# Gated linear attention and a bilinear FFN on one core: tokens put in order where y leaves PSUM, and a new order of all steps

## The chip, the cores and the metric

The kernel runs on one core of one Trainium2 chip. The metric is device time in microseconds (us) of the whole kernel, inputs and output in HBM, lower is better; it is given as the median of several runs.

The engines are named as in the profile: PE (matmuls; PEld its weight loads), DVE (vector), ACT (scalar), POOL (GpSimd) and SP (the engine that only issues DMAs here).

## The reference

Two stages. The first is a recurrence over 768 positions for each of 4 batches and 8 heads, with a state of 48 x 48; the second is a bilinear FFN on the 3072 tokens that come out of it.

```python
def _attn_ref(q, k, v, alpha):               # each (4, 8, 768, 48)
    state = np.zeros((B, H, D, D))
    for t in range(S):
        state = alpha[:, :, t, :, None] * state + np.einsum('bhd,bhe->bhde', k[:, :, t], v[:, :, t])
        y[:, :, t] = np.einsum('bhd,bhde->bhe', q[:, :, t], state)

def _moe_ref(x, w_a, w_b, w_out):            # x (3072, 384), w_a, w_b (384, 1536), w_out (1536, 384)
    return (x @ w_a) * (x @ w_b) @ w_out
# x = y, transposed to (batch * position, head * 48)
```

## The kernel before

The work is cut into six chunks. A chunk covers two batches and 256 positions: batches 0 and 1 in the even chunks, 2 and 3 in the odd ones, and chunks 0 and 1, 2 and 3, 4 and 5 share their positions. A chunk gives 512 tokens to the FFN. Inside a chunk, `u` (0 or 1) is the batch and `g` (0 or 1) is the half of 128 positions. Two neighbouring positions share a partition when q, k, v and alpha are loaded (r = 0 or 1), so that a half has 64 partitions and the attention's own order of tokens in a half is (r, s), first all even positions and then all odd ones. Within a half the recurrence is done in matmul form (scores between queries and keys, masked, times v), and between halves a state is carried.

Nothing is scheduled by a compiler. A text, `PROGRAM`, lists all steps in one order with their chunk in front (`1: a 2 0 3` is step `a` of chunk 1), and a loop at the end of the kernel calls the function of each step. Every engine executes its own instructions strictly in that order, and semaphores make it wait for the others. The last digits of a PE step name the PSUM bank, of which there are eight of 512 columns; a step that takes a bank waits until its last reader has finished. Letters at the end of a step name the engine: V is DVE, S is ACT, P is POOL, Y is SP. `*` in place of a digit means both batches of the chunk (full width, 512 tokens); a digit means one (half width, 256).

The steps that the text below speaks of:

- `ld` loads q, k, v or alpha; `W` and `Wo` load the FFN's weights. Loads on POOL's queue are issued by GpSimd, on Y by SP.
- `ln`, `ra`, `l2`, `l2s`, `R`, `H`, `L` prepare the logarithms of alpha; `B`, `A2`, `AQ` are PE's cumulative sums of them (L591, L592, L633, L638); `E` are the exponentials on ACT (L667); `lv` multiplies q or k by one of them; `mq` and `mk` (L678, DVE) write the scaled queries and keys into QKp.
- `C` transposes QKp on PE (L736) and `Ce` evicts it to kqT (chunks 0 and 1); `T` does the same with a DMA transpose issued by SP (chunks 2 to 5, L767).
- `D` are the scores (L841), which read kqT; `M` masks them on DVE (L846), `Mc` copies them on ACT (L850) and `Mm` masks that copy on DVE (L854).
- `v` casts v (L785 on ACT, L787 on DVE); `K` and `K2` are the key-value products (L799, L812) and `k` updates the state on DVE; `dk`, `de`, `dr`, `dl` bring the decay of a half to where `k` reads it.
- `SB`, `SA` and `Y` add up y in two banks (L865): the parts that come from the carried state and the part inside a half. `X` (L900, L902) evicts y from PSUM into xT.
- `a` and `b` (L919) multiply a block of 128 columns of w_a or w_b with xT, `as` (L925, ACT) evicts `a`, `pr` (L933, DVE) multiplies it with `b` out of PSUM into `prod`; `o` and `oc` (L941, L952) multiply by w_out, `ot` and `otc` (L956, L958) evict, `st` and `stc` store.

Attention matmuls use a quarter of PE's array each (64 x 64), four at a time; the transposes and the FFN use the whole of it. PE's steps of different chunks stand between each other in `PROGRAM`, so that the FFN of one chunk runs while the next chunk's attention is prepared on the other engines.

Up to the change, `X` evicts both halves of a batch with one instruction and keeps the order (r, s) of the columns; `a` and `b` read 512 columns in a row; and `pr` puts the tokens in order, by writing every second element of `prod`.

Of the kernel before, what the change touches and what calls it, by code (L numbers as in the profile page):

```python
# [101 lines left out]
1: as 2 0
0: ot 2 S
1: pr 4 0
2: R 1; lv 1 q P
1: b 3 0 6; b 2 0 7; a 5 0 2; pr 3 0; b 5 0 3; as 5 0; b 1 0 5; a 1 0 1; pr 5 0; pr 2 0; a 7 0 2; as 1 0; pr 1 0
2: AQ 3
1: SB 1 6
2: lv 0 k P
1: a 10 0 5  # L110
2: lv 1 k V; ra 0; ld v * P
1: Mm 1 1 V
2: E 1 b
1: as 10 0; b 10 0 0; pr 10 0
2: mq 1 V; E 1 i
1: as 7 0; b 7 0 1
2: E 0 b; E 0 i
1: a 0 0 5
0: st 3 Y
2: dr  # L120
1: SA 1; Y 1
2: mk 1 V
1: pr 7 0; a 11 0 0; a 6 0 3; b 6 0 2; X 1 S; b 11 0 4; a 2 1 6; as 6 0; a 3 1 7; as 11 0; b 2 1 1; pr 6 0
2: lv 0 q V
1: b 4 1 0; as 2 1
2: T 1
1: pr 11 0
2: dl
0: st 0 Y
1: a 0 1 2; pr 2 1  # L130
2: mq 0 V
1: b 3 1 3; b 0 0 6; as 3 1; as 0 0; b 0 1 7; pr 3 1; a 8 0 1; a 9 0 5
0: st 1 Y
1: b 8 0 3; b 9 0 4; pr 0 0; as 0 1
2: mk 0 V
1: a 4 1 2
3: ln *
1: a 9 1 6; pr 0 1; as 8 0; b 9 1 1
3: ra 1
1: b 10 1 7; pr 8 0; a 10 1 3; as 4 1; as 9 0; as 9 1; a 6 1 6; b 6 1 2; b 11 1 5; pr 4 1; as 10 1; pr 9 0; a 11 1 4; pr 10 1; pr 9 1; as 6 1  # L140
2: v 1 S
1: a 8 1 3; b 8 1 1; a 7 1 6; pr 6 1
3: l2 0 V
1: as 11 1
2: T 0
1: as 8 1; a 5 1 4
3: ra 0
1: as 5 1; a 1 1 2
2: v 0 V
4: ld a * Y  # L150
1: pr 11 1; as 7 1; pr 8 1
2: K2 * * 0 7; D 1 1 3; D 1 0 5
1: as 1 1; b 5 1 2; o 2 0 1
2: k * 0 V
1: pr 5 1
3: v 0 S; v 1 S
1: b 1 1 2
2: Mc 1 0; M 1 1
3: l2s 0 P; l2s 1 P
1: b 7 1 0; o 2 1 -; pr 1 1; o 3 0 4  # L160
2: SB 0 5
1: pr 7 1
3: R 0
2: D 0 0 2
1: ot 2 V
2: Mm 1 0 V
1: o 3 1 -
2: Mc 0 0; SB 1 0; D 0 1 2
3: R 1
1: ot 3 S  # L170
2: SA 0
1: o 0 0 4
0: cs 0 0 P
2: Mc 0 1
4: ln *
3: ld q * Y; ld k * Y
2: k * 1 V
3: AQ 2
2: Y 1; SA 1; Mm 0 1 V; Mm 0 0 V; Y 0; X 0 S
3: E 0 b  # L180
4: l2 0 V
2: X 1 V
1: o 0 1 -
2: b 1 * 6; a 1 * 5
3: E 1 b
# [48 lines left out]
3: D 1 0 1; D 1 1 3
2: as 10 *
3: k * 1 V; Mc 1 1
2: o 0 0 7; o 2 0 0
3: M 1 0
5: ln *
2: pr 10 *  # L240
4: lv 1 q P
3: SB 1 3; D 0 1 1; Mc 0 1
4: lv 1 k P
5: ld q * Y
1: st 0 Y
3: SB 0 5
2: o 2 1 -
3: Mm 1 1 V; Mm 0 0 V; Mm 0 1 V
4: ld v * P
2: ot 2 S; o 0 1 -  # L250
4: AQ 0; E 0 b; E 0 i
3: SA 0; Y 0; SA 1
4: E 1 b
3: Y 1
5: l2s 1 V
4: mq 0 V; mk 0 V
3: X 0 S; X 1 S
2: o 3 0 2; o 3 1 -
4: T 0
3: a 5 * 3  # L260
4: E 1 i; v 0 S
3: a 9 * 0
2: ot 3 S
3: b 5 * 6; a 6 * 5; as 5 *
2: st 2 Y
3: as 9 *
5: ld k * P; l2s 0 P
3: as 6 *
5: ra 1
# [12 lines left out]
3: b 1 * 7; as 1 *; a 3 * 5; b 9 * 6; pr 9 *; b 6 * 4; a 2 * 0; pr 6 *
4: T 1
5: lv 0 k P
3: b 0 * 6; as 0 *; as 2 *
4: dl
3: a 8 * 1
5: lv 1 q P
3: b 4 * 0; a 4 * 4; b 2 * 3; pr 1 *; pr 0 *; as 8 *; pr 2 *; as 4 *; pr 4 *; b 3 * 6; b 8 * 2
5: ld v * P; lv 1 k P  # L290
3: a 11 * 1
5: ra 0
3: as 3 *; pr 8 *; as 11 *; a 7 * 0
4: D 1 0 3; K * 0 5
5: lv 0 q P
3: pr 3 *; as 7 *
5: v 1 V
4: k * 0 V
5: R 1
4: D 1 1 6; D 0 1 1; Mc 1 0; Mc 1 1; M 0 1  # L300
2: o 1 0 0; o 1 1 -
3: a 10 * 7; b 11 * 3
4: SB 1 4
2: ot 1 S
3: as 10 *
# [72 lines left out]
5: b 11 * 1
# [26 lines left out]
def kernel(  # L405
# [11 lines left out]
    nc = tc.nc  # L417
# [681 lines left out]
```

## Time and profile before

| | |
|---|---|
| Three runs | 193.74, 194.33, 194.84 us; median 194.33 us |
| Profiled execution, first to last instruction (span) | 192.0 us, which is 2.3 us under the median; the profile gives no other time for this execution |
| PE, DVE, ACT, POOL busy | 186.8, 133.1, 106.5, 56.9 us |
| Granted TensorE clock | 1.00 over the span, full from 6.0 us after the start on |
| HBM read, written | 25.98 MB, 4.74 MB |
| DMA transposes | 8, issue to landing 4.3 to 5.9 us |
| Last matmul ends | 188.65 us |

The profile is of one execution. Its page has the busy time of each engine, the span in 40 slices, the DMA queues, the chain of waits that ended last, the costliest groups of instructions (line, engine, operation, written tile, read tiles, shapes, count; then busy time and the mean ns of one; then the idle time of the engine ahead of them and what ended it) and the DMA issues with their time to landing. The trace behind it answers further: the pieces of the chain in order of time (start, length, what), a timeline (start, length, engine, line, operation, and in brackets the idle time of the engine before it), groups by form, and the instructions of one line or tile.

### The profile page before, as it was taken

Reading aid. Unit: us, or ns where it says so; the run is one execution under the profiler, and the core shown is the slowest. Engines: PE = TensorE matmul, PEld = TensorE weight load, DVE = VectorE, ACT = ScalarE, POOL = GpSimd, SP = SyncE. Lnnn points to the kernel's source line nnn. Section 1 sums busy time; section 2 is a strip of 40 time slices with the busy share of each in tenths; the row PEclk is TensorE's granted clock in tenths of the full one; section 3 lists DMA queues with packets and bytes.
Section 4 is the critical chain, followed back from the end, with each engine's and each line's share of the span. In section 5 each row is a group of like instructions: output and inputs, shape, how many; then the busy total and the mean of one; then the engine's idle time right before and its main releaser. Section 6 shows DMA issues by size and latency. Waiting matters only on the chain.

```text
span 192.0 us, 6086 instructions
## 1 busy us (share of the span) xinstructions
PE 186.8 (97%) x2613; PEld 116.9 (61%) x2613; DVE 133.1 (69%) x223; ACT 106.5 (55%) x194; POOL 56.9 (30%) x75
## 2 busy tenths in 40 slices
PE   7999999999999999999999999999999999999992
PEld 3888875677778876645557444656465644545562
DVE  2387698994989888899897956887567446252510
ACT  4448885656779867753487756743572435314211
POOL 8999626752450500640074262000000000000000
PEclk9999999999999999999999999999999999999999
DMA  5999999999969999999999989017641200000422
GB/s 132 274 219 218 251 253 235 244 269 264 251 107 166 165 216 265 248 254 149 233 213 181 156 174 129 3 42 140 146 66 44 85 0 0 0 0 3 164 82 82
DMA packets 62618, 29.40 MB, mean 153 GB/s; under 512 B 53712, under 2 KB 60768, under 8 KB 62592
## 3 DMA queue, kind: packets, MB, share of 16 engines
q0 software_dynamic: 18432, 13.37, 39.6%
q1 hardware_dynamic: 44016, 15.55, 38.1%
q8 instruction: 20, 0.33, 0.7%
q10 hardware_dynamic: 144, 0.10, 0.2%
q14 instruction: 6, 0.05, 0.1%
HBM read 25.98 MB, written 4.74 MB: 160 GB/s over the span
## 4 chain that ended last, share of the span: by engine, by line
PE 91%; DMA 5%; SPq 1%; DVE 1%; issue 1%; ACT 0%; DVEq 0%
PE psum L919 47%; PE psum L941 24%; PE psum L865 7%; PE psum L841 3%; DMA kqT<-QKp 3%; DMA q_t<-in_q_dram 3%; PE psum L736 2%; PE psum L633 1%; PE psum L952 1%; SPq L549 1%; PE psum L799 1%; PE psum L812 1%; PE psum L700 1%; PE psum L591 1%; PE psum L592 1%
## 5 line engine op out<-in xcount | busy, mean ns | idle before, releaser
L919 PE MATMUL psum<-xT,wb_t 128*128 128x512 bf16 (+1 forms) x270 | 56.0, 337 | 0.0
L919 PE MATMUL psum<-xT,wa_t 128*128 128x512 bf16 (+1 forms) x270 | 56.0, 337 | 0.0
L941 PE MATMUL psum<-wo_t,prod 128*128 128x384 bf16 x276 | 49.4, 326 | 0.0
L919 PEld LDWEIGHTS <-wb_t 128*128 128x128 bf16 x270 | 25.9, 98 | 19.9 <-issue 0.5
L919 PEld LDWEIGHTS <-wa_t 128*128 128x128 bf16 x270 | 25.9, 98 | 19.7 <-issue 0.3
L941 PEld LDWEIGHTS <-prod 128*128 128x128 bf16 x276 | 25.9, 98 | 17.6
L956 ACT ACTIVATE ot<-psum 128x384 f32<-128x384 f32 (+1 forms) x16 | 7.7, 482 | 22.7 <-PE psum L941 21.6
L850 ACT ACTIVATE m<-psum 128x1024 bf16<-128x1024 f32 x14 | 14.1, 1023 | 4.6 <-PE psum L841 4.3
L613 POOL TENSOR_TENSOR l<-la 64x384 f32<-64x384 f32 x7 | 7.8, 1108 | 26.6 <-ACT la L556 19.0
L846 DVE TENSOR_TENSOR m<-psum,mask 128x1024 bf16<-128x1024 f32 x10 | 12.1, 1220 | 3.1 <-PE psum L841 3.1
L652 POOL TENSOR_TENSOR q_t<-q_t,ra 128x384 f32<-128x384 f32 x5 | 6.1, 1215 | 22.5 <-ACT ra L645 19.7
L556 ACT ACTIVATE la<-a_t 128x1536 f32<-128x1536 f32 (+2 forms) x9 | 9.5, 1055 | 2.3 <-DMA a_t<-in_alpha_dram 2.2
L678 DVE TENSOR_TENSOR QKp<-q_t,beta 128x768 bf16<-128x768 f32 x10 | 10.0, 995 | 1.0 <-ACT beta L667 1.0
L865 PE MATMUL psum<-m,vx 64*64 64x128 bf16 x576 | 10.5, 217 | 0.0
L900 ACT ACTIVATE xT<-psum 128x768 bf16<-128x768 f32 x9 | 7.2, 816 | 5.7 <-PE psum L865 5.5
L678 DVE TENSOR_TENSOR QKp<-k_t,invb 128x768 bf16<-128x768 f32 x10 | 9.7, 972 | 0.8 <-ACT invb L667 0.8
L854 DVE TENSOR_TENSOR m<-m,mask 128x1024 bf16<-128x1024 bf16 x14 | 9.3, 684 | 1.2 <-ACT m L850 1.2
L958 DVE COPY ot<-psum 128x384 f32<-128x384 f32 (+1 forms) x9 | 4.8, 532 | 7.6 <-PE psum L941 4.7
L865 PEld LDWEIGHTS <-vx 64*64 64x64 bf16 x576 | 9.0, 107 | 0.5 <-issue 0.3
L841 PE MATMUL psum<-kqT 64*64 64x128 bf16 x384 | 9.0, 219 | 0.4 <-DMA kqT<-QKp 0.3
L652 POOL TENSOR_TENSOR k_t<-k_t,a_t 128x384 f32<-128x384 f32 x6 | 7.4, 1228 | 6.1 <-issue 3.3
L549 POOL DMA_DIRECT2D v_t<-in_v_dram x8 | 8.5, 1058 | 0.1
(271 smaller groups left out, 287.9 us busy)
## 6 DMA issues: line engine op xcount, KB each, us to landing
out_dram<-ot SPq DMA_DIRECT2D x23, 192.0 KB, 3.8
q_t<-in_q_dram SPq DMA_DIRECT2D x3, 768.0 KB, 6.5
a_t<-in_alpha_dram POOLq DMA_DIRECT2D x2, 768.0 KB, 15.2
k_t<-in_k_dram POOLq DMA_DIRECT2D x2, 768.0 KB, 12.1
v_t<-in_v_dram POOLq DMA_DIRECT2D x4, 384.0 KB, 7.0
a_t<-in_alpha_dram SPq DMA_DIRECT2D x2, 768.0 KB
k_t<-in_k_dram SPq DMA_DIRECT2D x2, 768.0 KB
a_t<-in_alpha_dram POOLq DMA_DIRECT2D x3, 384.0 KB, 8.5
```

The costliest lines, as they stand in the source:

```text
L549: eng.dma_start(out=t[:, us, hs].rearrange("p b h r d -> p (b h) (r d)"), in_=src[ch.b0 + us.start:ch.b0 + us.stop, hs, ch.s * 2 * C:(ch.s ...
L556: nc.scalar.activation(out=ch.la[:, us, hs].rearrange("p b h r d -> p (b h r d)"), in_=ch.a[:, us, hs].rearrange("p b h r d -> p (b h r d) ...
L613: eng.tensor_add(ch.l2[(1 - g) * HC:(2 - g) * HC, 1], x[:, :, 0, :], x[:, :, 1, :])
L652: eng.tensor_mul(x, x, by)
L678: eng.tensor_mul(QKp[ch.c % 2][:, u, j, :, hs, :D], src[:, u, hs].rearrange("p h r d -> p r h d"), f)
L841: nc.tensor.matmul(s2[g * HC:(g + 1) * HC, r, p, rk, :], lhsT=turned_part(ch, u, 1, rk, 2 * h + p, g, rs), rhs=queriesT(ch, u, 2 * h + p, ...
L846: nc.vector.tensor_mul(m.rearrange("p r a k s -> p (r a) (k s)"), ch.s2[u, h].rearrange("p r a k s -> p (r a) (k s)"), maskn(4))
L850: nc.scalar.activation(out=m.rearrange("p r a k s -> p (r a) (k s)"), in_=ch.s2[u, h].rearrange("p r a k s -> p (r a) (k s)"), func=AF.Copy)
L854: eng.tensor_mul(x, x, maskn(4))
L865: nc.tensor.matmul(y[c * DP:(c + 1) * DP, g, j // 2 * C:(j // 2 + 1) * C], lhsT=lhsT, rhs=rhs, start=(g, c) not in begun, stop=False, skip ...
L919: nc.tensor.matmul(p, lhsT=(wa_t, wb_t)[w][:, kk, f * 128:(f + 1) * 128], rhs=ch.xT[:, kk, us, :], start=(kk == 0), stop=(kk == KT - 1))
L941: nc.tensor.matmul(op, lhsT=ch.prod[:, f, at:at + C], rhs=wo_t[:, f, :], start=(f == 0), stop=(f == NFF - 1))
```

## The change

The eviction `X` now takes one half `g` at a time, `X u g engine`, 384 columns each, and writes them in order of tokens: the reading side goes through PSUM in a row and the writing side takes every second element. xT is laid out by half (128 partitions x 4 halves x 3 blocks of 128 rows x 128 tokens), so the moving operand of a full `a` or `b` comes in four pieces of 128 columns, of a half-width one in two. `pr` then has three plain operands, and the two functions that made views for it are gone.

```diff
-    def evac(ch, u, eng):
+    def evac(ch, u, g, eng):
         if not hasattr(ch, "xT"):
-            ch.xT = wk.tile([128, KT, B, C], BF16, name="xT")
-        o_ = ch.xT[:, :, 2 * u:2 * u + 2, :].rearrange("p a g s -> p g a s")
-        i_ = ch.y[u][0][:, :, :KT * C].rearrange("p g (a s) -> p g a s", a=KT)
-        if eng is nc.scalar:
-            nc.scalar.activation(out=o_, in_=i_, func=AF.Copy)
-        else:
-            eng.tensor_copy(o_, i_)
+            ch.xT = wk.tile([128, B, KT, C], BF16, name="xT")
+        evict(ch.xT[:, 2 * u + g].rearrange("p a (s r) -> p a r s", r=2),
+              ch.y[u][0][:, g, :KT * C].rearrange("p (a r s) -> p a r s", a=KT, r=2), eng)
...
-    def tokens(x, us):
-        return x.rearrange("p (b s r) -> p b r s", s=HC, r=2)[:, us]
-
-    def columns(x, n):
-        return x.rearrange("p (b r s) -> p b r s", r=2, s=HC)
...
-            nc.tensor.matmul(p, lhsT=(wa_t, wb_t)[w][:, kk, f * 128:(f + 1) * 128], rhs=ch.xT[:, kk, us, :], start=(kk == 0), stop=(kk == KT - 1))
+            nc.tensor.matmul(p, lhsT=(wa_t, wb_t)[w][:, kk, f * 128:(f + 1) * 128], rhs=ch.xT[:, us, kk, :], start=(kk == 0), stop=(kk == KT - 1))
...
-        o_, a_, b_ = tokens(ch.prod[:, f, :], us), columns(a[:, :n], n), columns(b, n)
-        nc.vector.tensor_mul(o_, a_, b_)
+        nc.vector.tensor_mul(ch.prod[:, f, us.start * C:us.stop * C], a[:, :n], b)
```

`PROGRAM` is new as a whole. It has the same steps with three differences: 24 evictions `X` (17 on ACT, 7 on DVE) in place of 12 (9 and 3); the casts of v are 6 on ACT and 6 on DVE, by batch, instead of 9 and 3; and some evictions changed engine (`ot` 17 on ACT and 6 on DVE instead of 15 and 8, `otc` both on ACT instead of one each, `Ce` 3 on ACT and 5 on DVE instead of 2 and 6). The order, the PSUM banks and the place of the transposes among the other steps are different throughout. The beginning, and the parts with the DMA transposes of chunks 2 and 4:

```diff
-0: ... fill 7 2; cu2 V; cz 0 q V; cus; ld k 0b Y; ld k 0a Y; B 0b 5; ld q 0b Y; ld v 0 P
-0: ln 0a; ld q 0a Y; E 0b b; E 0b i; mq 0b V; B 0a 0; E 0a i; dk 0 2; E 0a b; ld a 1 P; mk 0b V; C 0 1 5; ... v 0 S; mk 0a V; cm 1
-0: de 0; fill 2 1; mq 0a V; C 0 0 3; Ce 0 1 V; ... Ce 0 0 V; D 0 1 4; ln 1; ... K 0 0 6; k 0 0 V; M 0 1; D 0 0 0; SB 0 6
-0: cz 1 q P; B 1a 2; ...
+0: ... c1; fill 7 0; cz 0 q V; ln 0a; ci; ld k 0b Y; ld k 0a Y; cu; cu2 V; cus; cz 1 b P; B 0b 2
+0: E 0b i; mk 0b V; E 0b b; ld q 0b Y; B 0a 0; ld v 0 P; mq 0b V; dk 0 2; ld q 0a Y; C 0 1 3; fill 2 4; E 0a b; mq 0a V; E 0a i; mk 0a V; ld a 1 P; C 0 0 0; v 0 S
+0: K 0 0 1; cs 0 m P; Ce 0 1 V; D 0 1 4; Ce 0 0 V; D 0 0 6; ld k 1 P; de 0; ld q 1 P; k 0 0 V; cm 1; M 0 0; SB 0 0; M 0 1; W b 0 256; ln 1; B 1a 2; E 1a b
...
-2: mk 1 V
-1: pr 7 0; a 11 0 0; a 6 0 3; b 6 0 2; X 1 S; ...
-2: T 1
...
-2: mk 0 V
...
-2: T 0
...
-2: K2 * * 0 7; D 1 1 3; D 1 0 5
...
-2: D 0 0 2
+2: mk 1 V
+1: a 6 0 3; a 11 0 0; ...
+2: mk 0 V
...
+2: mq 0 V
...
+2: dr; v 0 V; T 1; K2 * * 4 5
+1: pr 8 0; as 6 1
+2: D 1 0 1; Mc 1 0
...
+2: T 0
...
+2: D 1 1 6; M 1 1; D 0 0 2; Mc 0 0
...
-4: mq 0 V; mk 0 V
-3: X 0 S; X 1 S
-2: o 3 0 2; o 3 1 -
-4: T 0
-3: a 5 * 3
...
-4: D 0 0 3
+4: mk 0 V; T 0
+3: a 9 * 3; as 9 *
...
+4: D 0 1 4; M 0 1
```

GpSimd's queue holds the same list of instructions in the same order as before.

More of the change, by code (lines that the diff above doesn't have):

```diff
@@ new lines @@
+0: as 3 0; pr 3 0
+1: ld v 0 P; l2 1 V
+0: b 3 1 0; pr 3 1
+1: ld q 1 P
+0: Wo 0 6
+1: ld k 1 P
+0: a 5 1 2; as 0 1; pr 0 1; a 10 * 3; as 10 *; Wo 6 12; b 10 * 0; b 11 * 5
+1: H 1 V; L 1 V
+0: pr 10 *
+1: E 0 i; dk * 3
+0: as 11 *; pr 11 *
+2: ld a * P
+0: as 5 1
+1: lv 0 q V
+0: pr 5 1; b 1 1 0; a 2 1 2
+1: A2 1 5
+0: a 1 1 7
+1: de *; ld v 1 P
+0: a 6 * 3
+1: E 1 i; E 1 b
+0: b 6 * 6; as 1 1
+1: lv 0 k V; mk 0 V
+0: pr 1 1; a 7 * 5
+1: E 0 b
+0: b 2 1 0
+1: v 0 S
+0: as 2 1; a 9 * 4; as 6 *; as 9 *
@@ new lines @@
+2: ld q * P
+1: mq 0 V; C 0 1 7
+0: pr 2 1; pr 6 *
+1: Ce 0 1 S
+0: b 9 * 0; pr 9 *; b 7 * 4; as 8 *
+1: K2 0 0 2 3; k 0 0 V
+2: ld k * P
+0: as 7 *; pr 7 *
+1: D 0 1 6; M 0 1
+0: o 0 0 0
+1: C 0 0 1
+0: b 8 * 2; pr 8 *; o 1 0 4
+1: ra 1; lv 1 q V
+3: ld v * P
+1: Ce 0 0 S; SB 0 6
+0: cz 1 v P
+1: lv 1 k P; mk 1 V
+0: c3 P
+1: D 0 0 1; Mc 0 0
+0: o 0 1 -; o 2 0 5
+3: ld a * P
+1: mq 1 V; C 1 1 1
+0: ot 0 S
+1: C 1 0 0
+0: o 2 1 -
+1: Mm 0 0 V
+2: ln *; ra 1
+0: cs 1 0 P
+1: Ce 1 0 S; k 0 1 V; Ce 1 1 V
@@ new lines @@
+0: o 1 1 -; ot 1 S
+2: l2s 0 P
+0: ot 2 S
+1: SA 0; Y 0; X 0 1 S; X 0 0 S
+2: l2 0 V
+1: v 1 V
+2: l2s 1 P
+1: D 1 1 0; Mc 1 1; K2 1 1 2 3
+0: o 3 0 4; o 3 1 -
+1: a 10 0 5; as 10 0; a 3 0 0
+2: ra 0
+1: D 1 0 6; as 3 0
+0: ot 3 S
+2: R 0; R 1
+1: k 1 0 V; k 1 1 V
+2: AQ 1; E 0 i
+1: b 3 0 3; a 1 0 0; as 1 0; M 1 0
+0: st 3 Y
+1: pr 3 0; b 1 0 4; pr 1 0; b 10 0 5; pr 10 0; SB 1 6; Mm 1 1 V
+2: lv 1 q P; E 1 b; mq 1 V; lv 1 k V; lv 0 k P
+1: a 5 0 0; as 5 0; b 5 0 3; pr 5 0
+2: E 0 b
+1: a 4 0 4; b 7 0 5; as 4 0
@@ new lines @@
+2: SB 1 4
+1: pr 11 1
+2: D 0 1 6
+3: l2 0 V; R 0; R 1; ld q * Y
+2: Mc 0 1; Mm 0 1 V
+4: ln *
+1: o 3 0 1; o 3 1 -; ot 3 V
+2: Mm 0 0 V
+3: AQ 6
+4: l2 0 V
+3: E 1 b
+2: SA 1; Y 1; X 1 0 S
+4: l2s 0 P
+3: v 1 V
+2: SA 0
+3: ld k * Y; lv 0 k P
+4: ld k * Y
+2: Y 0; X 0 0 V
+1: o 0 0 1; o 0 1 -
+3: E 0 b
+1: st 3 Y
+3: dr
+2: X 0 1 S; X 1 1 S; a 1 * 2; as 1 *; b 1 * 3
+4: ld q * Y
+3: E 0 i
+2: a 3 * 4; b 2 * 2
+1: ot 2 S
+2: a 4 * 0
+3: lv 1 k V; lv 0 q P; mq 0 V
+2: a 2 * 5; as 2 *
+3: E 1 i
+2: b 3 * 6
@@ new lines @@
+3: lv 1 q V; dl
+2: pr 1 *
+3: mk 0 V
+2: b 11 * 3; pr 2 *; b 4 * 5; a 11 * 2
+4: l2s 1 P
+2: a 9 * 7
+0: st 2 Y
+2: as 4 *; as 11 *; b 9 * 0
+3: mk 1 V; T 0; mq 1 V; T 1
+2: pr 4 *
+5: ld a * Y
+2: pr 11 *
+4: R 0
+2: b 6 * 2
+1: ot 0 V
+2: a 8 * 5; as 9 *; pr 9 *
+4: ra 1
+2: a 7 * 3; a 6 * 7; as 3 *; pr 3 *; as 6 *; pr 6 *
+1: o 1 0 4
+2: as 8 *
+4: lv 1 q P
+3: K2 * * 0 1
+5: ld q * Y
+3: k * 0 V; D 0 0 6; Mc 0 0; k * 1 V
+2: a 0 * 2
+1: st 2 Y
+2: as 7 *; as 0 *; b 8 * 5; pr 8 *
+1: o 1 1 -; ot 1 V
@@ new lines @@
+2: b 7 * 0; pr 7 *; a 10 * 1
+3: Mm 0 0 V; SB 1 2; D 1 1 4; D 1 0 6; M 1 0
+2: as 10 *; b 0 * 0; pr 0 *
+3: Mc 1 1
+2: a 5 * 1; as 5 *; b 5 * 4
+4: lv 0 k V
+3: SB 0 6; SA 1
+2: pr 5 *
+4: lv 1 k P
+3: D 0 1 0
+2: b 10 * 5
+3: Mc 0 1
+2: o 2 0 4
+3: Mm 1 1 V; Y 1
+4: R 1; AQ 0; E 0 b; ld v * P
+3: Mm 0 1 V
+4: v 0 S
+3: Y 0
+2: pr 10 *
+3: X 1 1 S; X 1 0 V; SA 0; X 0 1 V; X 0 0 S
+4: E 1 i; mk 1 V; E 0 i
+1: st 0 Y
+4: E 1 b; ra 0; lv 0 q V; mq 0 V
+2: o 2 1 -; o 0 0 5
+5: ln *
+3: a 3 * 2
+4: mk 0 V; T 0
@@ new lines @@
+3: a 9 * 3; as 9 *
+4: v 1 V
+3: b 4 * 0
+4: mq 1 V
+2: ot 2 V
+5: l2s 1 V; l2 0 V
+3: a 11 * 1
+2: o 3 0 6
+3: a 4 * 3
+2: o 0 1 -
+5: ld k * P
+3: as 11 *
+4: dr
+3: a 6 * 1; b 9 * 4; pr 9 *; as 6 *; b 11 * 7; pr 11 *
+2: ot 0 S
+3: a 7 * 1; b 3 * 4
+5: l2s 0 P
+3: as 3 *; pr 3 *; b 6 * 2; pr 6 *
+5: R 0; R 1
+3: b 1 * 7; a 1 * 4; as 1 *; as 4 *; a 8 * 2; a 0 * 5
+5: ra 1
+2: st 2 Y
+4: T 1
+3: pr 4 *
+5: lv 0 k P
+3: b 0 * 4; b 5 * 3; pr 1 *; as 0 *; pr 0 *; a 5 * 0; b 8 * 7; as 5 *; pr 5 *
@@ new lines @@
+3: as 10 *; pr 10 *
+2: st 3 Y
+5: E 1 i; mk 1 V
+4: a 3 * 1
+3: pr 7 *; o 3 1 -
+4: a 6 * 3; b 0 * 6
+5: v 0 V
+4: as 7 *; as 6 *
+2: st 0 Y
+3: o 2 0 4
+4: a 0 * 3; as 0 *
+5: mq 1 V; T 0
+4: pr 7 *; pr 0 *; pr 6 *; as 3 *; a 1 * 2; as 1 *; b 3 * 7; pr 3 *; a 4 * 3; as 4 *
+3: o 2 1 -; ot 2 S
+4: b 1 * 1; pr 1 *
+5: T 1; D 1 1 2; D 1 0 4
+3: ot 3 S
+5: D 0 0 6; M 1 0; Mc 0 0; K * 0 0; dl; k * 0 V; Mm 0 0 V
+3: o 1 0 1; o 1 1 -; ot 1 V
+5: SB 0 4; SB 1 6; Mc 1 1; D 0 1 2; M 0 1; Mm 1 1 V
+3: st 2 Y
@@ new lines @@
+3: st 1 Y
+4: as 2 *; b 2 * 7; b 5 * 0; pr 2 *; pr 5 *
+5: b 3 * 2; a 3 * 7
+4: o 3 0 0
+5: as 3 *; pr 3 *
+4: o 0 0 1
+5: b 0 * 2; as 0 *; pr 0 *; as 1 *; b 1 * 3; b 9 * 6
+4: o 1 0 2; o 1 1 -
+5: a 6 * 7
+4: o 0 1 -
+5: pr 1 *; b 6 * 3; as 5 *; b 5 * 4
+4: ot 1 S
+5: b 7 * 2
+4: o 3 1 -; ot 0 S; st 0 Y
+5: as 6 *
+4: ot 3 V; st 3 Y; o 2 0 7; o 2 1 -
+5: pr 5 *; o 0 0 4; as 7 *; a 9 * 5; a 10 * 0; pr 7 *; pr 6 *; b 10 * 1; as 10 *; pr 10 *
+4: ot 2 S
+5: as 9 *
+4: st 1 Y
+5: o 3 0 2; oc 1 1 0 3; o 2 0 5
@@ L401 @@
+4: st 2 Y
+5: pr 9 *; o 0 1 -; ot 0 S; st 0 Y; o 3 1 -; ot 3 S; oc 1 1 1 -; otc 1 1 S; o 2 1 -; ot 2 S; st 3 Y; st 2 Y; stc 1 1 S; oc 1 0 0 0; oc 1 0 1 -; otc 1 0 S; stc 1 0 Y
 """
```

427 lines of the change are left out of this document (86 added, 341 removed).

## The prediction

> **What bounds the kernel now.** I read the page's busy time and slices first, then the groups by form, then the chain of waits in order of time, then the timeline of the first 20 us.
>
> ```profile
> span 192.0 us, 6086 instructions
> PE 186.8 (97%) x2613; PEld 116.9 (61%) x2613; DVE 133.1 (69%) x223; ACT 106.5 (55%) x194; POOL 56.9 (30%) x75
> PE   7999999999999999999999999999999999999992
> ```
>
> PE is busy in every slice but the first and the last; no other engine passes 69%. A busy PE is not yet a PE at its rate, so I price its work from the chain of waits, whose pieces run from one matmul's end to the next:
>
> ```profile
> 19.34 3.41 PE psum L919 x30
> 28.04 0.35 PE psum L638 x2
> 72.50 0.29 PE psum L865 x12
> 100.74 0.17 PE psum L865 x12
> 106.47 4.99 DMA kqT<-QKp
> 135.85 5.18 PE psum L919 x24
> ```
>
> 24 full-width matmuls take 5.18 us, 0.216 each, so a full `a` or `b` step (three) costs 0.65 us and a half-width one 0.33. Twelve quarter-array matmuls cost 0.17 us behind others of their kind and 0.29 behind whole-array work, so each change of kind costs about 0.11. With such prices (output half 0.98, scores step 0.23, `Y` 0.68) I add up PE's steps in the order of the program: 182.05 us. The clock of the trace minus this sum is then the time PE has lost so far. It is 5.53 us at 28.04 (`A2` of chunk 1), 5.59 at 102.96 (`AQ` of chunk 4), 5.86 at 111.50, and 6.60 at the last output matmuls. So PE loses 5.5 us at the start, nothing for 75 us, 0.3 at one wait, and 0.7 in crumbs behind it. That wait is a DMA transpose:
>
> ```profile
> 111.50 0.42 PE L841 MATMUL psum<-kqT 64*64 64x128 bf16 x16 [0.29 <-DMA kqT<-QKp]
> ```
>
> **PE's own work.** The two built programs hold the same 2,549 matmuls in the same shapes, with the same 49 changes between whole- and quarter-array work; the sum in the new order is again 182.05 us. Nothing is gained or lost there, unless the moving operand of `a` and `b`, which now comes in pieces of 128 columns, streams slower. The trace has such a pair: scores (L841) read two pieces of 64 columns and `Y` (L865, m) one of 128; their means are 219 and 217 ns. Over 540 matmuls 2 ns would be 1.1 us, the upper end; both have a median of 216, and I take 0. A gain is excluded: the same columns pass.
>
> **The eviction of y.**
>
> ```profile
> L900 ACT ACTIVATE xT<-psum 128x768 bf16<-128x768 f32 x9 | 7.2, 816 | 5.7 <-PE psum L865 5.5
> L902 DVE CAST xT<-psum 128x768 bf16<-128x768 f32 x3 | 2.9, 952 | 2.4 <-PE psum L865 2.4
> L956 ACT ACTIVATE ot<-psum 128x384 f32<-128x384 f32 x15 | 7.4, 492 | 21.7 <-PE psum L941 21.6
> L958 DVE COPY ot<-psum 128x384 f32<-128x384 f32 x8 | 4.4, 554 | 4.7 <-PE psum L941 4.7
> ```
>
> Nine ACT instructions of 0.816 and three on DVE of 0.952 become 17 of about 0.492 and 7 of about 0.554 (the output evictions have the new size): +1.0 us of busy time on each engine. Off the path, if the lead covers it: I count PE's work between the last matmul into y and the first `a` or `b` that reads xT. Before, the shortest lead is 0.70 us (chunk 0, `X 1`), under the 0.82 that the eviction takes, so up to 0.15 is lost there. After, the shortest is 1.10, with ACT and DVE taking one half each (0.55), and elsewhere 1.7 to 3.4: nothing is lost. No row of ACT shows writes in steps of two elements. From below 0.492; from above twice the time per element, 0.84 ns x 384 = 0.32 more (slope between 816 and 492); I take the lower end, nearest to DVE's interleaved products below. Even 0.81 fits into 1.10. The price is then 5.4 us of ACT time, which has 45% free; 0.5 us on the path is my upper end.
>
> **The products.** `pr` writes in a row instead of interleaved.
>
> ```profile
> L829 DVE TENSOR_TENSOR tmp<-psum,S 128x384 f32<-128x384 f32 x4 | 2.2, 552 | 1.2 <-PE psum L812 0.7 <-PE psum L799 0.6
> L829 DVE TENSOR_TENSOR tmp<-psum,Sm 128x192 f32<-128x192 f32 x4 | 1.4, 353 | 0.1
> L933 DVE TENSOR_TENSOR prod<-as__704,psum 128x512 bf16<-128x512 bf16 x1 | 0.7, 733 | 0.0
> ```
>
> Plain DVE work with one operand in PSUM has 1.04 ns per element and 0.154 fixed (552 and 353), so 0.683 for 512 against 0.733 now. 54 x 0.045 + 36 x 0.02 = 3.2 us of DVE time fewer. Three casts of v leave ACT (0.85 each) for DVE (0.35). DVE is 9.6 of 10 us busy between 80 and 90 us, so this can remove crumbs, 0 to 0.5 us; I take 0.2. The Trainium skill (SBUF — State Buffer, Door 1: The DMA port swizzle) says that accesses run at full rate while they hit the same 16-byte line again, so that bf16 may be strided by up to 8 elements for free. By it the interleaved writes cost nothing, the products stay at 0.73 and the 0.2 is nil. The rows differ by 7%, though of other shapes, and I go by the rows.
>
> **The start.** `mk 0b` now comes ahead of `mq 0b`:
>
> ```profile
> 7.81 0.56 DVE L678 TENSOR_TENSOR QKp<-q_t,prod 128x384 bf16<-128x384 f32 x1 [3.63 <-DMA q_t<-in_q_dram]
> 8.94 0.62 PE L736 MATMUL psum<-ident,QKp 128*128 128x128 bf16 x8 [0.15 <-DVE QKp L678]
> 10.80 0.84 ACT L556 ACTIVATE la<-a_t 128x768 f32<-128x768 f32 x1 [0.43 <-DMA a_t<-in_alpha_dram]
> 12.03 0.59 PE L591 MATMUL psum<-la,ut 128*128 128x192 f32 x2
> 12.86 0.77 POOL L529 DMA_DIRECT2D wb_t<-in_moe_w_b_dram  x1
> wb_t<-in_moe_w_b_dram POOLq DMA_DIRECT2D x1, 384.0 KB, 7.6
> ```
>
> k has landed while DVE waits for q, so the four products end about 0.3 earlier; `K 0 0` in front of the scores waits for v's cast (10.12), which gives some back. `B 1a` can start at 11.65 (10.80 + 0.84) instead of 12.03: 0.35 gained. But `b 5 0` needs w_b's columns 256 to 768, which land at 12.86 + 7.6 = 20.45; GpSimd's queue has the same order. In the new order 15.14 us of PE work stand before it, so PE has lost at least 5.3 there, restart included 5.35: 0.2 of the 0.35 remain.
>
> **The transposes.** `T 0` of chunk 4 had 6.05 us of PE work between its last product `mk 0` and the first scores that read it; now 13.7. The 0.3 of the one wait goes. What is late next: chunk 2's two transposes, whose lead falls from 10.6 and 10.0 us to 7.55 and 6.9. Less the product itself (0.95), 6.6 and 5.95 remain; before, issue to landing took 4.4 and 5.9 there (all eight: 4.3 to 5.9). It just fits: 0. Chunk 5's shortest lead rises from 2.3 to 3.7, where DVE has run ahead of the order. The queues of SP and GpSimd keep nearly their order (a store fewer ahead of chunk 2's second transpose; three stores ahead of chunk 5's two instead of two between them, 0.4 us each to issue, hidden by that lead).
>
> **The end.** The last store moves from ACT's queue to SP's, which must be woken: +0.05.
>
> **Sum.** -0.2 (start) -0.3 (transpose) -0.2 (crumbs) +0.05 = -0.65 on a span of 192.0. The span lies 2.3 us under the median of 194.33; with the same 2.3 the forecast is **193.7**.
>
> **Rivals.** *A. More:* all crumbs go, since DVE is lighter and evictions start by halves; PE then ends 5.4 us behind its sum instead of 6.6: -1.2, 193.1. For it: 75 us without a loss in the trace. Against: the crumbs lie where chunk 4 and 5 hand over, and the new order has them too.
>
> *B. The products don't get shorter* and DVE takes up 1.0 us for evictions and 1.05 for v: crumbs come back as large as the gains, 194.3, no change. For it: the cited rule. Against: 733 over 683.
>
> *C. Slower:* chunk 2's transposes come late. PE's next scores stand behind them in order, and each us past 5.95 from issue to landing costs PE one. For it: 5.9 was seen at that very place, and four large loads follow in SP's queue. At 8 us: +2.0 - 0.65, 195.7. Against: 4.4 for the first of the two.
>
> **Numbers.** Forecast (193.7, own range 193.3 to 194.2) 0.45; A 0.22; B 0.18; C and other losses, such as slower streaming or ACT writes, 0.15. The range 192.9 to 195.2 takes in A, B and the cheap half of C. About 0.5%, 1 us, can be told from no change: faster takes A and the low edge of the forecast, 0.30; slower takes most of C and a tail of B, 0.17; within 0.53.
>
> **What would show it.** In the new profile: PE without a wait on kqT past 100 us; products near 0.69; xT evictions of 0.49 and 0.55; B 1a at 11.65; the last matmul at about 188.0. Wrong it is if PE waits on kqT near 64 or 69 us, if full-width matmuls take more than 0.216, or if DVE's products stay at 0.73.

## The result and the profile after

The changed kernel takes 196.19 us (median of four runs, 195.96 to 197.11), the kernel before 194.06 (also four runs). The ratio is 1.0117, with a 95% interval of 1.0079 to 1.0155: the change costs 2.1 us. The forecast was 193.7 with a range of 192.9 to 195.2, so the result lies outside, on the slow side. The profiled execution took 195.96 us with a span of 194.2, and the last matmul ends at 191.15 instead of 188.65.

The page of the changed kernel, first the busy time:

```profile
span 194.2 us, 6085 instructions
PE 187.6 (97%) x2612; PEld 116.7 (60%) x2613; DVE 136.3 (70%) x226; ACT 105.6 (54%) x203; POOL 57.2 (29%) x75
```

DVE should have become lighter, since its 90 products are shorter now. It is 3.2 us busier. The groups by form show that the products did what was forecast, and that ACT's evictions are longer:

```profile
L906 ACT ACTIVATE xT<-psum 128x384 bf16<-128x384 f32 x17 | 9.2, 599 | 5.2 <-PE psum L826 5.1
L883 DVE TENSOR_TENSOR prod<-as__1915,psum 128x512 bf16<-128x512 bf16 x1 | 0.7, 681 | 0.0
```

So something else on DVE has grown. What PE waits for is listed in the waits of PE (line, what ended the wait, us in total, times, longest; the first row, a wait at the very start that the kernel before has too, and the last one are left out):

```profile
...
PE psum L870 <- DVE ot L908: 0.7, 1, 0.7
PE psum L826 <- issue: 0.5, 1, 0.5
PE psum L870 <- ACT as__486 L876: 0.4, 1, 0.4
PE psum L870 <- DMA wa_t<-in_moe_w_a_dram: 0.3, 1, 0.3
PE psum L870 <- DVE prod L883: 0.2, 1, 0.2
...
```

The wait for a DMA transpose at 111.5 us, the only large one of before, is not in this list; a wait of 0.7 for DVE has come in its place. The timeline around it, DVE, GpSimd and PE in turn (start, length, instruction):

```profile
109.63 1.16 DVE L748 COPY vx<-v_t 128x768 bf16<-128x768 bf16 x1
110.71 1.75 DVE L639 TENSOR_TENSOR QKp<-q_t,beta 128x768 bf16<-128x768 f32 x1
112.39 0.54 DVE L908 COPY ot<-psum 128x384 f32<-128x384 f32 x1
...
108.97 1.60 POOL L574 TENSOR_TENSOR l<-la 64x384 f32<-64x384 f32 x1 [14.78 <-ACT la L517]
110.66 0.99 POOL L613 TENSOR_TENSOR k_t<-k_t,a_t 128x384 f32<-128x384 f32 x1
...
112.98 1.46 PE L870 MATMUL psum<-xT,wb_t 128*128 128x512 bf16 x6 [0.69 <-DVE ot L908]
```

The same two instructions at other places of the same trace, with no GpSimd instruction beside them:

```profile
77.99 0.34 DVE L748 COPY vx<-v_t 128x768 bf16<-128x768 bf16 x1
...
87.33 0.94 DVE L639 TENSOR_TENSOR QKp<-q_t,beta 128x768 bf16<-128x768 f32 x1
```

The cast of v takes 1.16 us instead of 0.34, and the queries' product 1.75 instead of 0.94. Both start while a product of GpSimd runs, and they end 0.22 and 0.81 after that product's end (110.57 and 111.65), about what they take by themselves: they have stood until then. DVE loses 1.6 us here, its next eviction is that much late, and PE, which needs the evicted bank, stands for 0.69.

To find all such places I compared each DVE instruction with the shortest one of the same line, tiles and shape in the same trace and added up what it had more, where that was over 0.12 us. In the kernel before this gives 2.4 us, in the changed kernel 7.2. Without it DVE would be busy 130.7 us before and 129.1 after, lighter as forecast. Nine instructions of the changed kernel stand for 0.65 to 0.82 each; all overlap a product on GpSimd. Four of the nine lie between 45 and 53 us, where PE does not wait at all, so there it cost nothing. DVE instructions with an operand in PSUM, some forty of which overlap GpSimd's products in the two traces, have at most 0.03 more.

What that is to PE is seen in two stretches, 70 to 90 and 90 to 115 us (columns: length, then busy us and instructions of PE, PEld, DVE, ACT, POOL). First the kernel before, then the changed one:

```profile
70.00:90.00 20.00, 20.00 (x277) 11.17 (x276) 18.32 (x27) 11.77 (x20) 5.23 (x4) 1.00 1.12 241
90.00:115.00 25.00, 24.71 (x401) 13.50 (x400) 20.85 (x29) 15.99 (x27) 10.39 (x9) 1.00 1.02 189
```

```profile
70.00:90.00 20.00, 19.52 (x288) 11.06 (x287) 16.78 (x25) 12.71 (x23) 5.84 (x5) 1.00 1.11 217
90.00:115.00 25.00, 24.13 (x384) 13.32 (x383) 22.91 (x34) 13.75 (x23) 6.79 (x6) 1.00 0.97 189
```

Before, PE lost 0.29 in these 45 us, after, 1.35. The last matmul ends 2.50 us later than before. These 45 us give 1.07 of that, of which 0.46 is the wait named "issue", which no semaphore explains. Another 0.6 is idle time in the first 30 us, which differs from one execution to the next (see below), and 0.8 is PE's busy time itself, 187.6 instead of 186.8 us; what makes it longer was not found.

### The profile page after: what moved, and what is told of

It reads as the page before. It is cut to its first block, busy times and chain, and to the rows that moved or that the text cites. A ratio compares the mean times of both kernels' runs of the same rounds, so it can differ in the third digit from the quotient of the medians.

```text
span 194.2 us, 6085 instructions
## 1 busy us (share of the span) xinstructions
PE 187.6 (97%) x2612; PEld 116.7 (60%) x2613; DVE 136.3 (70%) x226; ACT 105.6 (54%) x203; POOL 57.2 (29%) x75
## 5 line engine op out<-in xcount | busy, mean ns | idle before, releaser
L870 PE MATMUL psum<-xT,wb_t 128*128 128x512 bf16 (+1 forms) x270 | 56.8, 337 | 1.1 <-DVE ot L908 0.7
L891 PE MATMUL psum<-wo_t,prod 128*128 128x384 bf16 x276 | 49.9, 326 | 0.0
L574 POOL TENSOR_TENSOR l<-la 64x384 f32<-64x384 f32 x7 | 9.2, 1307 | 38.9 <-ACT la L517 34.2
L906 ACT ACTIVATE ot<-psum 128x384 f32<-128x384 f32 (+1 forms) x19 | 8.8, 473 | 14.6 <-PE psum L891 14.0
L906 ACT ACTIVATE xT<-psum 128x384 bf16<-128x384 f32 x17 | 9.2, 599 | 5.2 <-PE psum L826 5.1
L639 DVE TENSOR_TENSOR QKp<-q_t,beta 128x768 bf16<-128x768 f32 x10 | 10.5, 1045 | 1.9 <-ACT invb L628 1.8
L815 DVE TENSOR_TENSOR m<-m,mask 128x1024 bf16<-128x1024 bf16 x14 | 10.2, 737 | 1.2 <-ACT m L811 1.2
L613 POOL TENSOR_TENSOR q_t<-q_t,ra 128x384 f32<-128x384 f32 x5 | 5.4, 1077 | 17.0 <-ACT ra L606 16.4
L908 DVE COPY ot<-psum 128x384 f32<-128x384 f32 x6 | 3.3, 549 | 6.4 <-PE psum L891 6.4
```

The lines of the kernel that those rows point to most:

```text
L574: eng.tensor_add(ch.l2[(1 - g) * HC:(2 - g) * HC, 1], x[:, :, 0, :], x[:, :, 1, :])
L613: eng.tensor_mul(x, x, by)
L639: eng.tensor_mul(QKp[ch.c % 2][:, u, j, :, hs, :D], src[:, u, hs].rearrange("p h r d -> p r h d"), f)
L815: eng.tensor_mul(x, x, maskn(4))
L870: nc.tensor.matmul(p, lhsT=(wa_t, wb_t)[w][:, kk, f * 128:(f + 1) * 128], rhs=ch.xT[:, us, kk, :], start=(kk == 0), stop=(kk == KT - 1))
L891: nc.tensor.matmul(op, lhsT=ch.prod[:, f, at:at + C], rhs=wo_t[:, f, :], start=(f == 0), stop=(f == NFF - 1))
```

## The experiments

The theory to be tested, called P below: DVE instructions that read and write only SBUF stand still while GpSimd works on a product; the new order puts more of them there. Its rivals: the new eviction costs (E), DVE is simply loaded too much (L), the weights land later (W). The results in one table; "standing" is the sum described above, "PE busy" is of the 45 us from 70 to 115, both in the one execution that was profiled. Each ratio is to runs of the kernel before that were taken with it; their median is 194.06 down to "six products to DVE" and 193.96 below it.

| Kernel | Median, us | Ratio to before (95%) | Standing, us | PE busy, us |
|---|---|---|---|---|
| before | 194.06 | | 2.4 | 44.71 |
| changed | 196.19 | 1.0117 (1.0079 to 1.0155) | 7.2 | 43.65 |
| eviction alone | 194.06 | 0.9998 (0.9980 to 1.0016) | 2.3 | 44.56 |
| order alone | 196.02 | 1.0093 (1.0072 to 1.0115) | 6.5 | 43.52 |
| first FFN steps swapped | 196.63 | 1.0120 (1.0096 to 1.0144) | 5.7 | 43.36 |
| six products to DVE | 197.52 | 1.0187 (1.0148 to 1.0226) | 3.4 | 41.95 |
| the same, loads held back | 195.86 | 1.0088 (1.0067 to 1.0109) | 3.2 | 44.40 |
| half an output step moved | 196.17 | 1.0120 (1.0094 to 1.0146) | 5.9 | 43.15 |
| GpSimd cleared | 194.75 | 1.0039 (1.0020 to 1.0058) | 2.1 | 44.45 |
| cleared, half step moved | 194.56 | 1.0032 (1.0018 to 1.0046) | 2.7 | 45.00 |
| before, one product to DVE | 194.13 | 1.0008 (0.9991 to 1.0024) | 3.0 | 44.93 |
| before, dummy products | 195.13 | 1.0059 (1.0038 to 1.0081) | 4.6 | 43.84 |
| before, dummy memsets | 193.89 | 0.9998 (0.9986 to 1.0009) | 2.4 | 44.66 |

Neither column alone puts the kernels in the order of their times: where DVE stands and what PE meets at the start count too.

**Which half of the change.** The first kernel is the one before, in its own order, with only the eviction by halves, the new xT and the plain products (the functions as in the change):

```diff
-0: ... X 0 S; ...
+0: ... X 0 0 S; X 0 1 S; ...
```

> The kernel before, in its own order, with the new eviction alone: X by halves in the order of tokens (each X u e becomes X u 0 e; X u 1 e), xT by halves, plain products. Theory P with W (the order costs, by collisions of DVE with GpSimd and by weights that land later): 193.7 to 194.5, no change, products 0.68, xT evictions on ACT 0.60, on DVE 0.59. Rival E: the eviction costs, 195 or more, with PE gaps in front of the first a or b of each chunk.

It is level with the kernel before. ACT's evictions take 0.607 (18 of them) and PE waits once for one, 0.2. The eviction costs nothing and gains nothing; E falls.

The second has the changed kernel's order with the old eviction, one `X u e` where the later half stood, the old xT and the interleaving products:

```diff
-2: SA 1; Y 1; X 1 0 S
+2: SA 1; Y 1; X 1 S
```

> The changed kernel's order with the eviction of before: one X for a batch at the place where its later half stood, xT in its old layout, interleaving products. Theory P with W: the order alone brings the loss, 195.7 to 197 (products 0.05 us longer each, DVE busier by 3), PE gaps near 77, 93 and 113 us again. Rival E: 194.3, as before the change.

By the medians it brings 1.96 of the 2.1 us. Cast and queries' product are long again:

```profile
109.59 1.16 DVE L748 COPY vx<-v_t 128x768 bf16<-128x768 bf16 x1
110.67 1.75 DVE L639 TENSOR_TENSOR QKp<-q_t,beta 128x768 bf16<-128x768 f32 x1
```

The new `PROGRAM` alone makes the loss. Its order and its choice of engines, such as the casts that went from ACT to DVE, are not told apart by this.

**The start.** The waits for `wa` and the one named as ACT's `as` at 21.1 us looked like weights that land late:

```diff
-0: ... SB 1 6; a 1 0 0
-0: as 1 0; a 5 0 2; as 5 0; a 4 0 1; b 1 0 3; pr 1 0; as 4 0; b 5 0 4; b 0 0 5; a 3 0 0; ... a 0 0 1; pr 5 0
+0: ... SB 1 6; a 5 0 0
+0: as 5 0; a 1 0 2; as 1 0; a 4 0 1; b 1 0 3; pr 1 0; as 4 0; b 0 0 5; a 3 0 0; ... a 0 0 1; b 5 0 4; pr 5 0
```

> The changed kernel with another order of the first FFN steps of chunk 0: a 5 ahead of a 1 (w_a's columns 256 to 768 land first), b 0, a 3 and a 0 ahead of b 5 (w_b's columns 256 to 768 land last). Theory W: PE's gaps at 19.5 (0.41 beyond a change of kind) and 21.4 us (0.48) are waits for these landings, which other steps now cover: -0.8, 195.4. Rival: the second gap is a wait for ACT's eviction of a 4, as the profile names it; then it stays and the gain is 0.3 or less, 195.9.

Both waits are gone from its trace, and it is no faster; W falls as a cause. The waits at the start differ from one execution to the next: with one and the same start the wait for `wb` was 0 in the kernel with half an output step moved and 1.3 in the one with the loads held back. In the first 30 us PE is busy 27.0 to 28.4 us in five profiled executions with the start of before, and 26.7 to 28.4 in seven with the new one; the means are 27.76 and 27.67.

**GpSimd's products away.** Six products that stood beside the long DVE instructions go to DVE:

```diff
-4: l2s 0 P        +4: l2s 0 V
-4: l2s 1 P        +4: l2s 1 V
-4: lv 1 q P       +4: lv 1 q V
-4: lv 1 k P       +4: lv 1 k V
-5: l2s 0 P        +5: l2s 0 V
-5: lv 0 k P       +5: lv 0 k V
```

> Against the changed kernel (196.2 us) only six small GpSimd products (l2s of chunk 4 twice and of chunk 5 once, lv 1 q and lv 1 k of chunk 4, lv 0 k of chunk 5) go to DVE. Theory P (port): DVE instructions with all operands in SBUF stand still while GpSimd works; the four that did so between 76 and 112 us (0.75, 0.81, 0.70, then 0.82 and 0.81 us too long) cost PE 0.53 + 0.12 + 0.23 + 0.74 = 1.6 us. Then these PE gaps (77.5, 85.5 and 87.0, 93.7, 113.4) are gone, DVE takes six times 0.55 more and some 3.9 less, and the time is about 194.6. Rival E (the new eviction is what costs): 196.2, the gaps elsewhere. Rival L (DVE is simply loaded too much): 3.3 us more on DVE makes it slower, over 196.7.

Slower, and not for any reason on the list. The cast takes 0.35 again and the queries' product 0.95, as P has it, but PE waits elsewhere, as the timelines of DVE and of PE show:

```profile
113.40 0.35 DVE L748 COPY vx<-v_t 128x768 bf16<-128x768 bf16 x1
113.67 0.95 DVE L639 TENSOR_TENSOR QKp<-q_t,beta 128x768 bf16<-128x768 f32 x1
...
95.06 0.42 PE L802 MATMUL psum<-kqT 64*64 64x128 bf16 x16 [2.48 <-DMA kqT<-QKp]
```

GpSimd, with less to do, starts the loads of v and k at 82.10 and 88.04 instead of 91.83 and 93.02, and chunk 3's first transpose, issued at 85.4, lands only at 95.0. In the changed kernel it was issued at 86.0 and landed 5.6 us later. So GpSimd's products had also held its loads back. Behind this wait the trace has something that no other profile here shows: the granted clock of PE is 0.50 from 95.92 to 99.33 us. This execution is the slowest of its six (199.54 us, median 197.52), and the other five list a mean clock of 0.999 or 1.0 instead of 0.991, so the median holds less than this trace shows.

The next kernel holds them back by a copy of one element that reads the finished transpose:

```diff
+3: gatet 0
 4: R 1; AQ 0; E 0 b; ld v * P
```

> The same six GpSimd products on DVE as in the run before, and one tiny GpSimd copy that reads kqT of chunk 3's batch 0 ahead of the load of v of chunk 4, so that the two loads on GpSimd's queue start as late as in the changed kernel (91.8 and 93.0 us) and not at 82.1 and 88.0, where they ran into chunk 3's transposes (landing 95.1, PE idle for 2.5 us). Theory P: the wait at 95 goes and the gaps at 85, 87, 94 and 113 us (0.12, 0.23, 0.74) stay away: 1.1 under the changed kernel, 195.1; the gap at 77.4 stays (next run). Rival L: DVE's 3.3 us more bring new gaps of the same size: 196.2.

The waits at 85 to 113 stay away, and a new collision takes half of the gain, with a product that had been left on GpSimd (118.94 to 119.93); the timeline of DVE and of PE:

```profile
119.10 1.24 DVE L614 TENSOR_TENSOR k_t<-k_t,a_t 128x384 f32<-128x384 f32 x1
...
120.99 0.81 PE L871 MATMUL psum<-xT,wb_t 128*128 128x512 bf16 x3 [0.49 <-DVE prod L884]
```

The gain is 0.3 instead of the expected 1.1, so this kernel alone settles nothing about P. It differs from the one before it by nothing but the later loads, and the wait at 95 is gone: the loads had delayed the transpose.

**The gap without a releaser.** PE stands 0.5 at 77 us in the middle of `Y 1` of chunk 2 with no semaphore to explain it ("issue"). Two kernels ask about it:

```diff
-0: ... fill 2 4; ...
+0: ... warm 8 4; ...
```

> The changed kernel with 8 dummy matmuls of 128 columns in the place of 2 of 512, at 9.6 us, about as long, so that every later PE instruction stands 12 places further down (6 weight loads, 6 matmuls). Theory F (fetch): the gap of 0.53 at 77.3 us comes in the middle of chunk 2's Y 1, behind its 33rd matmul and without a releaser, in four kernels of this order at PE's 2497th instruction, give or take one: it is the edge of a block of 256 instructions that PE fetches by DMA and that is not there yet. Then it comes six matmuls earlier, behind the 27th. Rival M: the 34th matmul waits for its operand (a mask by DVE): the gap stays behind the 33rd. Time as the changed kernel, 196.2.

Neither came: the gap is gone from `Y 1` altogether. The operands are the same, so a wait of the 34th matmul for its mask would have stayed. What comes instead is a wait of `Y 0` for a mask that stands beside a product of GpSimd (1.43 us instead of 0.68):

```profile
77.77 0.64 PE L826 MATMUL psum<-m,vx 64*64 64x128 bf16 x32 [0.28 <-DVE m L815]
```

In the kernel with six products moved and the loads held back that mask takes 0.68 again, and the gap in `Y 1` is still there, with 0.60; M falls. In the DMA records the 16 KB block of instructions that is transferred around there starts at 72.8 us instead of 74.5. That speaks for the fetch. Against it, the place where the gap should have gone was forecast wrongly, and in the changed kernel that transfer is over at 75.75, a microsecond before the gap begins at 76.8. The cause of the gap stays open. This kernel was run once (196.84 us), too few to compare its time; it has a wait of 1.0 for `wb` at the start and one of 0.98 at 86, the latter the same as in the next kernel.

```diff
-2: SA 1; Y 1; X 1 0 S
+2: SA 1
+1: o 0 0 1
+2: Y 1; X 1 0 S; X 1 1 S
...
-1: o 0 0 1; o 0 1 -
+1: o 0 1 -
```

> The changed kernel with half an output step (o 0 0 of chunk 1, 0.98 us of PE work) between SA 1 and Y 1 of chunk 2 instead of behind Y 0, two evictions X moved along with it. Theory F: PE reaches the edge of the block a microsecond later, when it has been fetched: the gap of 0.53 goes, two changes of kind (0.22) come in, 195.9. Rival M: the gap moves along with Y 1 or the wait is somewhere else: 196.4.

The gap at 77 goes here too, and the time does not fall, because PE meets DVE again at 85, in its timeline:

```profile
85.26 1.46 PE L872 MATMUL psum<-xT,wb_t 128*128 128x512 bf16 x6 [0.97 <-DVE prod L885]
```

DVE had stood idle for 1.84 us until GpSimd's product of q was done (82.3), because `mq 0` stands in front of the products in its order, and then 0.8 longer in `lv 1 q` beside GpSimd. The changed kernel has both at the same place. Whatever PE gains before 85 it gives back there.

**GpSimd's products of chunks 4 and 5 away.** In the changed kernel, these and two of chunk 3 go to DVE, and the loads are held back as above (the lines that come to the six moved products and the copy shown above):

```diff
-3: ld k * Y; lv 0 k P
+3: ld k * Y
-3: lv 1 k V; lv 0 q P; mq 0 V
+3: lv 1 k V; lv 0 k V; lv 0 q V; mq 0 V
-5: lv 1 q P
+5: lv 1 q V
-5: lv 1 k P
+5: lv 1 k V
-5: lv 0 q P; mq 0 V; mk 0 V
+5: lv 0 q V; mq 0 V; mk 0 V
+4: gatet 1
 5: ld v * P; v 1 V
```

> The changed kernel with all of GpSimd's products of chunks 4 and 5 and the two lv of chunk 3's batch 0 on DVE (lv 0 k next to mq 0 there), and its loads behind tiny copies that read the finished transposes (chunk 3's batch 0, chunk 4's batch 1), so that they start about as late as in the changed kernel. Against the run with six moved products (195.9) the last collision (119.1, 0.7 on DVE, 0.54 on PE at 121.4) and DVE's wait of 1.8 for GpSimd's product at 82 go as well. Theory P: PE's gaps from 80 to 130 are changes of kind alone, what is left against the kernel before is the gap at 77.4 (0.6) less the wait at 111.5 (0.36): 194.5. Rival L (DVE takes the time back): 195.9 or more.

> The same with the half output step between SA 1 and Y 1 of chunk 2 as well. With it alone the gap of 0.53 at 77.4 went and came back as a wait of DVE at 85.3 (0.97), behind GpSimd's q of chunk 3; here that wait is gone. Theory P with F: 194.1, level with the kernel before. Rival: 194.5 or more, another wait comes next.

The first takes 1.44 us off the changed kernel's median, though DVE is given eleven products more to do; L falls. With the half output step moved as well, PE is never idle between 70 and 115 (the stretches as above):

```profile
70.00:90.00 20.00, 20.00 (x293) 11.35 (x292) 17.93 (x30) 13.13 (x24) 0.00 (x0) 1.00 1.12 225
90.00:115.00 25.00, 25.00 (x389) 13.71 (x388) 22.78 (x38) 14.07 (x23) 2.84 (x3) 1.00 0.99 194
```

The 0.2 between these two medians is within their intervals. The second was to be level with the kernel before, at 194.1; it is not, and its rival, 194.5 or more, came. Some 0.6 us stay between it and the kernel before; what they are was not found.

**The collision by itself.** Two kernels are the one before with nothing changed but dummy work on GpSimd, at a place where it is idle for 13 us:

```diff
-4: l2s 1 P
+4: l2s 1 P; dum p 6      # memset dz; six times dy = dz * dz, 128x384 f32
```

> The kernel before, with six dummy products of 128x384 (scratch times scratch, in SBUF) and one memset on GpSimd behind l2s 1 of chunk 4, where GpSimd has nothing to do from 83.9 to 97.2 us. Theory P: of DVE's instructions there, those with all operands in SBUF (mq 0, lh, mk, two lv, ll, between 84.6 and 91) each stand up to 0.8 us, 3 to 4.5 in sum, the products out of PSUM stay at 0.73; DVE is full there, so PE loses 2 to 3.5: 196 to 197.5. Rival (GpSimd's work does not touch DVE, the long instructions had other causes): 194.1.

```diff
-4: l2s 1 P
+4: l2s 1 P; dum m 14     # memset dz; fourteen memsets of dy
```

> The same place, with 15 memsets of 128x384 on GpSimd instead, about as long in all, which read nothing from SBUF. Theory P as the traces so far show it (memsets beside DVE: +0.00 to +0.15): no change, 194.1. Rival (any work of GpSimd stops DVE): as with the products, 196 or more.

With products, the timeline of DVE and then of GpSimd:

```profile
85.21 1.57 DVE L678 TENSOR_TENSOR QKp<-q_t,beta 128x768 bf16<-128x768 f32 x1
88.21 0.72 DVE L933 TENSOR_TENSOR prod<-as__1864,psum 128x512 bf16<-128x512 bf16 x1
...
84.91 7.37 POOL L1002 TENSOR_TENSOR dy<-dz 128x384 f32<-128x384 f32 x6
```

With memsets, the same two in the same place:

```profile
84.84 0.94 DVE L678 TENSOR_TENSOR QKp<-q_t,beta 128x768 bf16<-128x768 f32 x1
...
84.40 6.60 POOL L1004 MEMSET dy<- 128x384 f32 x14
```

Beside products, four DVE instructions (`mq`, `lh`, `mk`, `lv`) stand 0.60 to 0.64 each, 2.5 in sum, PE waits 0.55 and 0.52 behind them, and the kernel is 1.17 us slower. Beside memsets of nearly the same length nothing stands and nothing changes. The `prod` with an operand in PSUM has its usual 0.72 in both. The size was forecast too high (2 to 3.5 on PE), since six dummies ended at 92.3 and two of the six DVE instructions ran behind them.

**The same in the kernel before.** Its own wait for a transpose at 111.5 goes back to such a collision. The kernel with the eviction alone, and one product moved:

```diff
-5: ld k * P; l2s 0 P
+5: ld k * P
-5: l2 0 V
+5: l2s 0 V; l2 0 V
```

> The kernel before, with the new eviction (which alone gave no change), and one more edit: l2s 0 of chunk 5 goes from GpSimd to DVE, behind the scores of chunk 4. In the kernel before, this product (103.45 to 104.72 us on GpSimd) stopped DVE's mq 0 of chunk 4 for 0.43, which the transpose of these queries waits for, and PE then waited 0.29 for that transpose at 111.5. Theory P: mq 0 takes 0.95 again, the wait at 111.5 goes, 193.7. Rival: the transpose is late for another reason (transfers beside it): 194.1, no change.

The wait is gone from the trace, the time is not lower. The 0.3 is no more than the half-width of the interval, and a new collision of 0.78 came in at 80.7. No version beat the kernel before.

## Why the prediction was wrong

The step that failed is the one on DVE: "3.2 us of DVE time fewer ... so this can remove crumbs, 0 to 0.5 us; I take 0.2". The durations of the products were right, and their sum was taken for DVE's time. What the sum leaves out is that an instruction has another length beside GpSimd. The new order moved DVE's SBUF instructions under GpSimd's products, the cast of v in chunk 4 among them, which ACT had done before, and DVE stands 7.2 us instead of 2.4. Clearing chunks 4 and 5 and part of 3 took back 1.44 of the 2.1 us, though that kernel also took away a wait of 1.84 of DVE for GpSimd's q, so that the two are not told apart in this figure. The collision itself is shown by the kernel with dummy products. What makes up the rest, the gap named "issue" and PE's longer busy time among it, stays open, and the prediction had no term for either.

It could have been read before. The prediction compared the order of GpSimd's queue before and after, but did not lay GpSimd's instructions beside DVE's in time. These two groups of the kernel before, same line, same shape and both in SBUF, show the thing in their means:

```profile
L652 DVE TENSOR_TENSOR k_t<-k_t,a_t 128x384 f32<-128x384 f32 x4 | 3.0, 750 | 0.0
L652 DVE TENSOR_TENSOR q_t<-q_t,ra 128x384 f32<-128x384 f32 x5 | 2.8, 554 | 0.3 <-DMA q_t<-in_q_dram 0.3
```

One of the four takes 1.35 us, at 80.58: it starts under one product of GpSimd and ends under the next. The Trainium skill (SBUF — State Buffer, Who interferes with whom) has the rule: a VectorE instruction with two inputs in SBUF contends with a GpSimd instruction that reads SBUF and not with one that only writes it, copies in the two-port modes contend too, and whoever starts first holds the ports until its end. The traces agree: DVE's products beside GpSimd's are 0.6 to 0.8 us longer, the cast 0.81, beside memsets 0.00, with an operand in PSUM at most 0.03, and GpSimd's product at 108.97, which starts under one of DVE's, takes 1.60 instead of 0.99. That the cast runs in such a mode no trace states; its 0.44 ns per element, where plain DVE work takes 1.04, fits. It was the rule against this change, and the prediction weighed another one.

The other steps in turn:

- **PE's own work**: full-width matmuls of `a` and `b` have a mean of 379 ns before and after, so four pieces of 128 columns stream like 512 in a row. PE's busy time as a whole still grew by 0.8 us, where the prediction has nothing; in one execution each it is 186.6 with the eviction alone, 187.3 with the order alone, and 186.8 and 187.4 in the two cleared kernels. Why is open.
- **The eviction** was mis-sized on ACT, 0.599 instead of 0.492, inside the bounds given (0.492 to 0.81); on DVE it is 0.586 for 0.554. It is off the path as forecast: the kernel with the eviction alone is level.
- **The products** take 0.671 to 0.689, forecast 0.683. The Trainium skill's rule cited there (SBUF — State Buffer, Door 1: The DMA port swizzle), that such strides are free, does not hold in these rows: 0.73 against 0.68 on DVE, 0.599 against 0.490 on ACT. The second pair also differs in type, bf16 against f32, but ACT's old evictions of 768 bf16 elements in a row (0.816) lie on the line through those of 192 and 384 f32 elements (0.330 and 0.492), so it is the step. The 0.2 for crumbs is not there all the same, since the kernel with the eviction alone has the shorter products and does not gain.
- **The start**: `B 1a` runs at 11.61 (forecast 11.65), and nothing is kept of it on the mean of the executions (27.76 and 27.67 us busy in the first 30).
- **The transposes**: right. PE waits for none, chunk 2's land in 4.4 and 5.3 us, the 0.3 at 111.5 is gone. Rival C did not come.
- **The end**: the 0.05 for SP's queue is not seen. The last store starts 0.03 us after its eviction both times, on ACT before (189.05) and on SP after (191.55).
- **Rival B** had the right engine and the wrong reason: crumbs came back on DVE, though the products did get shorter. No rival held the mechanism, so the range ended at 195.2.

## What to carry to other kernels

When steps are reordered, lay the helper engine's instructions beside the main one's in time, not only in each queue's order: a DVE instruction that works in SBUF and starts under a GpSimd product cost up to 0.8 us more here, and the time grew where PE was close behind. A group whose mean is above that of another of the same shape is the sign of it. Taking work from GpSimd can start its loads earlier, so look at what they then run into.

## What the hardware showed beside this

- ACT takes 0.599 us to write 384 bf16 elements out of PSUM in steps of two elements; 384 f32 elements in a row take 0.490.
- With GpSimd's loads issued at 82.1 and 88.0 us, a DMA transpose issued at 85.4 landed at 95.0; with the loads at 91.8 and later it took 5.6 us.
- After an idle time of 2.5 us PE's granted clock was 0.50 for 3.4 us in one execution, and three full-width matmuls took 1.49 us there, where such a three takes 0.81 right after. Idle times of up to 1.3 us behind the start of the other profiles had no such effect.
- The DMA records hold 20 transfers of 16 KB on a queue of kind "instruction", one for some 260 of PE's matmuls and weight loads. A gap of 0.46 to 0.65 us without a releaser came at the same instruction of PE (the 2497th or 2498th matmul or weight load) in six kernels, and went away when all instructions behind were shifted by 12 places.
